# Second MLP product of the token mixer in five stretches per half, more output projections inside the attention loop, and the last attention units in pairs

## The chip, the cores and the metric

The kernel runs on one core of a Trainium2 chip. The metric is the device time of one execution in microseconds (us); smaller is better. A profiled execution also leaves a trace of every instruction of the five engines: TensorE (PE, with its weight loads as PEld), VectorE (DVE), ScalarE (ACT), GpSimd (POOL) and SyncE (SP, which starts nearly all DMAs here).

## The reference

```python
g = sigmoid((x * gate_w).sum(-1))                    # x: 2048 tokens x 640
# A: attention, 32 heads of 20, one key and value head for all
q = (x @ wq) -> 32 heads x 2048 x 20;  k = x @ wk;  v = x @ wv      # 2048 x 20
p = softmax(q k^T / sqrt(20)) over 2048 keys
a = concat_heads(p v) @ wo                           # 2048 x 640
# B: mixer MLP over the token axis, for each of 640 channels
h = layernorm(x)                                     # over channels
u = gelu(h^T w1 + b1)                                # 640 x 1728
b = (u w2 + b2)^T                                    # 2048 x 640
out = g * a + (1 - g) * b                            # all float32
```

## The kernel before, in words

**Precision.** Large products are made in three fp32r products of a high and a low part (high*high, high*low, low*high), so each block product is three matmuls. Splitting a tile into its parts is a copy (high) and a subtraction (low).

**Attention.** 2048 queries x 32 heads are cut into 32 groups n (512 queries, 4 heads); each group has 16 key blocks kb of 128 keys. A pair (n, kb) is a unit; there are 512. For a unit TensorE makes four score tiles of 128 keys x 512 queries (`qk`, L655, "s"), ScalarE takes the exponential of each (L658, tile p), and `pv_mm` (L682) multiplies the four p with the values into one PSUM bank o, four heads side by side as column tiles of 32. Ahead of that, every group needs the maximum of each query's scores: TensorE makes the scores a second time with queries on the partitions (`ms_next`, L474, "m") and VectorE reduces each 512-wide tile (L477). The maxima go through DRAM back into two rows of the q tile (`store_max`, `fetch_max`).

Score products need 60 or 62 of 128 rows of the array, so each uses one half of the rows, 0 to 63 or 64 to 127.

**The loop of stretches.** The list `ph` has 326 entries; `main(k, vs)` issues one, called a stretch here. Stretch k has b = k % 2. Half b of the array rows makes scores ("s" and "m", 10 or 11), while the other half makes fillers: the matmuls of 64 rows x 320 columns of the MLP and of the output projection, with an "m" or two at the end or beginning. `merged` lays the two lists together by fixed guesses (0.232 and 0.147 us). A stretch closes with the value products of one unit (k even) or two units (k odd), which use all rows. With more than 15 fillers a stretch follows the lists `MANY` (11 score products on half b), with 15 or fewer `FEW` (10 in the one-unit stretches, 11 in the two-unit ones, with one m more on the other half). Where the first unit of a two-unit stretch is the last key block of its group, its value products are put in the middle of the stretch (`parted`).

The fillers of one item (one output tile of 128 x 320) accumulate in the single PSUM bank g. Before the fillers of the other row half may write there, a one-element VectorE memset (`flag`, L668) signals that those of the last stretch are done. After the last filler of an item ScalarE takes the bank out (`done`: L514 in the first MLP product, L749 in the second, L869 in the projection).

- Stretches 0 to 107: first MLP product, 18 items of 6 stretches, 16 fillers in each (the first ten items ran before the loop).
- Stretches 108 to 299: second MLP product (`b2_jobs`, L741), 16 token blocks x 2 channel halves d. The sum runs over 1728 = 13 x 128 + 64 rows of w2. A product of 128 rows is two fillers, one in each half of the array; the 64 rows left over go to either half. That makes 81 fillers per item, in 6 stretches of 13 or 14.
- Stretches 300 to 325: output projection (`a_jobs`, L856) of 6.5 of the 16 token blocks, 15 fillers in each stretch.

**What a finished group leaves to do.** `pv_mm` of key block 15 copies the bank o to SBUF (ScalarE, L695, tile oc) and queues steps in `later`: `scale` (a VectorE transpose L698, "turn", a reciprocal L703 and a GpSimd product), `back` (VectorE transpose L710), `high` and `low` (GpSimd, then eight DMAs to o_scr). `settle` takes one step at a time. The two heavy ones, `scale` and `back`, are taken only by `settle(wide)` with wide true, at the end of a two-unit stretch.

**The tail.** After the loop 24 units are left, with no maxima to make. They run in the blocks of `BLOCKS`: each issues scores up to 2 (block of 3) or 4 (block of 2) tiles beyond its own units, with fillers (`tail_job`, L812) between, and then the value products of its units in a row. The fillers are the projections that the loop did not do: 5.5 whole blocks and, for the last four token blocks, the rows of the heads that are done. Scores use three PSUM banks and the p tiles are 14 here. The last four heads' part of the last four blocks follows at the end.

**Queues.** All engines run in the order in which the program issues (manual schedule). SP starts all loads and stores in order; the w2 chunks (four per token block, `w1_load`) are loaded four chunks ahead, and GpSimd splits them (L124, L125) when `w1_upto` asks for it, in four pairs of tiles that the next block reuses. Tail loads (`tail_load`) go to SP too.

Of the kernel before, what the change touches and what calls it, by code (L numbers as in the profile page):

```python
# [17 lines left out]
P = 128  # L18
# [13 lines left out]
BLOCKS = (3, 3, 2, 3, 3, 3, 3, 2, 2)  # L32
# [6 lines left out]
def mix_kernel(ctx: ExitStack, tc: tile.TileContext, A_x, A_wq, A_wk, A_wv, A_wo,  # L39
# [51 lines left out]
    def w1_load(n):  # L91
        while len(w1raw) < min(n, len(chunks)):
            c = len(w1raw)
            wr = w1r.tile([P, HS, P], F32, name="wr")
            if c < W2:
                fc, hf = chunks[c]
                rows = slice(hf * HS * P, (hf + 1) * HS * P)
                for o in range(0, P, P if fc < FC - 1 else FT):
                    fw = P if fc < FC - 1 else FT
                    nc.sync.dma_start(out=wr[:, :, o:o + fw],  # L100
                                      in_=B_w1[rows, fc * P:fc * P + fw].rearrange("(c p) f -> p c f", p=P))
            else:
                st, hf = chunks[c]
                cols = slice(st * P, (st + 1) * P)
                nf = min(HS, FC - 1 - hf * HS)
                nc.sync.dma_start(out=wr[:, :nf, :],
                                  in_=B_w2[hf * HS * P:(hf * HS + nf) * P, cols].rearrange("(c p) s -> p c s", p=P))
                if nf < HS:
                    for o in range(0, P, FT):
                        nc.sync.dma_start(out=wr[o:o + FT, nf, :], in_=B_w2[(FC - 1) * P:, cols])  # L110
            w1raw[c] = wr

    def w1_upto(n):
        while fetched[0] < min(n, len(chunks)):
            c = fetched[0]
            w1_load(c + 1)
            nf = HS if c < W2 else min(HS, FC - chunks[c][1] * HS)
            wr = w1raw[c][:, :nf, :]
            wh = w1p.tile([P, HS, P], F32R, name="wh")[:, :nf, :]
            wl = w1p.tile([P, HS, P], F32R, name="wl")[:, :nf, :]  # L120
# [319 lines left out]
    u0 = upool.tile([P, 2 * FC * HD2], F32R, name="u0")  # L440
    u_hi = [view(t, 0, FC) for t in (u0, slot[0])]
    u_lo = [view(t, FC * HD2, FC) for t in (u0, slot[0])]
    pp_pool = ctx.enter_context(tc.tile_pool(name="pp", bufs=12))
# [166 lines left out]
    def second():  # L610
        right.close()
        xp = ctx.enter_context(tc.tile_pool(name="xp", bufs=1, side="right"))
        extra_p.extend(xp.tile([P, NB], F32, name=f"p{i}") for i in range(2))
# [22 lines left out]
    def next_p():  # L636
        turn_p[0] += spare[0]
        i = turn_p[0] % 14
        return extra_p[i - 1] if 0 < i < 3 else pp_pool.tile([P, NB], F32, name="p")
# [36 lines left out]
    def pv_mm(u):  # L676
# [7 lines left out]
        if kb == NS - 1:  # L684
# [8 lines left out]
            if not direct:  # L693
                src = ev.tile([P, NB], F32, name="oc")
# [35 lines left out]

    def b2_jobs(st):
# [26 lines left out]

        return (lambda: None), [(steps(d), lambda d=d: done(d)) for d in range(2)]
# [16 lines left out]
    NA = NS - 9  # L776
    jobs = [(st, 0, D) for st in range(NA - 1, NS - 4)]
# [22 lines left out]
    def tail_job(n):  # L800
# [3 lines left out]
        ds = (1,) if st < NA else (0, 1)  # L804
# [33 lines left out]
    def a_jobs(st):  # L838
        hold = {}
        ds = (0,) if st == NA - 1 else (0, 1)  # L840
# [97 lines left out]
    b2 = [b2_jobs(st) for st in range(NS)]  # L938
    m = len(seq)
    seq += batches(b2, [3] * 2 * NS)  # L940
    for st in range(NS - 1):
        for j, n in ((0, 1), (1, 2), (2, 4)):
            seq[m + 6 * st + 3 + j][1].append(lambda c=W2 + 4 * (st + 1) + n: w1_upto(c))
    seq[-1][1].append(second)
    for c in range(DC):
        seq[m + 9 + 8 * c][1].append(lambda c=c: load_wo(c))
        seq[m + 11 + 8 * c][1].append(lambda c=c: split_wo(c))
    aj = [a_jobs(st) for st in range(NA)]
    seq[-6][1].append(aj[0][0])
    seq += batches(aj, [1] * (2 * NA - 1))  # L950
    ph = [(rows[1 - b], rest if b else [], done if b else []) for rows, rest, done in seq for b in range(2)]
    for i in range(8):
        ph[2 * (m + 6 * NS) + 2 + 3 * i][1].append(lambda i=i: tail_load(i))
# [30 lines left out]
    def main(k, vs):  # L984
# [25 lines left out]
        settle(wide)  # L1010
# [28 lines left out]
    for n in BLOCKS:  # L1039
# [29 lines left out]
        while len(loaded) < len(jobs) and len(loaded) - 8 not in waiting and (len(loaded) < 10 or v >= 501):  # L1069
# [61 lines left out]
```

## Time and profile before

| | before |
|---|---|
| time, median of 3 runs (lowest to highest) | 1690.6 us (1690.49 to 1690.65) |
| the profiled execution's own time | 1690.12 us |
| its span, first to last instruction | 1688.3 us |
| loop, first to last flag (326 stretches) | 182.9 to 1598.4 us |
| stretches 108 to 299, second MLP product | 654.3 to 1490.2 us |
| busy: PE, DVE, ACT, POOL | 99%, 86%, 70%, 34% of the span |

The span is 1.8 us shorter than the execution, which holds what lies before the first and behind the last instruction. The ends of matmuls are modelled, so the busy share of PE says only that it always has something in flight; how well it is used is read from the distance between starts. The flag memset stands once in each stretch, so the times of the flags cut the loop into stretches.

### The profile page before, as it was taken

How to read it: one execution, taken by the hardware profiler on the slowest of the kernel's cores; microseconds unless marked ns; L12 is line 12 of the kernel's file. 1: busy time of each engine (PE TensorE's matmuls, PEld its weight loads, DVE VectorE, ACT ScalarE, POOL GpSimd, SP SyncE). 2: the span in 40 equal slices, each digit the busy share in tenths (PEclk: the TensorE clock that was granted, in tenths of full speed). 3: DMA queues.
4: the chain of work that ended last, by engine and by line, in shares of the span. 5: the costliest groups of instructions: out<-in, count | busy, mean ns of one | idle time of the engine just before them, and what ended most of it. 6: DMA issues, size and time to landing. Idle time of an engine off the chain costs nothing.

```text
span 1688.3 us, 38969 instructions
## 1 busy us (share of the span) xinstructions
PE 1677.0 (99%) x14865; PEld 1098.7 (65%) x14865; DVE 1444.0 (86%) x2759; ACT 1189.0 (70%) x2349; POOL 571.4 (34%) x720
## 2 busy tenths in 40 slices
PE   9999999999999999999999999999999999999998
PEld 7899766666666666665655665565666566566676
DVE  6679889988998998998898999889889889989824
ACT  4444677777777777777777777777777777777764
POOL 6468555544555553221122212222211222011200
PEclk9999999999999999999999999999999999999999
DMA  7665322223232231121222212121112221255521
GB/s 210 203 181 145 84 68 69 77 64 83 59 77 77 59 76 55 51 67 41 63 70 59 62 39 68 56 62 55 39 54 57 60 63 33 56 141 162 150 91 45
DMA packets 174977, 136.44 MB, mean 81 GB/s; under 512 B 32793, under 2 KB 140982, under 8 KB 174790
## 3 DMA queue, kind: packets, MB, share of 16 engines
q1 hardware_dynamic: 174502, 133.62, 28.6%
q8 instruction: 117, 1.92, 0.5%
q14 instruction: 70, 0.57, 0.1%
q10 hardware_dynamic: 288, 0.33, 0.1%
HBM read 101.25 MB, written 31.65 MB: 79 GB/s over the span
## 4 chain that ended last, share of the span: by engine, by line
PE 94%; DVE 3%; issue 2%; SPq 1%; DMA 0%; ACT 0%; POOL 0%; POOLq 0%; DVEq 0%; ACTq 0%
PE o L682 28%; PE ms L474 12%; PE s L655 12%; PE g L741 10%; PE ms L655 9%; PE s L474 7%; PE g L910 6%; PE pp L294 4%; PE pu L584 3%; PE g L856 1%; DVE mp L477 1%; PE ms L812 1%; PE pt L286 0%; DVE ot L698 0%; PE g L812 0%
## 5 line engine op out<-in xcount | busy, mean ns | idle before, releaser
L477 DVE TENSOR_REDUCE mp<-ms 128x1 f32<-128x512 f32 x1081 | 708.8, 686 | 112.8 <-PE ms L474 94.4
L658 ACT ACTIVATE p<-s 128x512 f32<-128x512 f32 x1079 | 610.4, 615 | 200.7 <-PE s L655 145.9
L477 DVE TENSOR_REDUCE mp<-s 128x1 f32<-128x512 f32 x967 | 634.0, 683 | 38.5 <-PE s L474 38.4
L658 ACT ACTIVATE p<-ms 128x512 f32<-128x512 f32 x969 | 542.0, 607 | 168.5 <-PE ms L655 140.9
L682 PE MATMUL o<-p,v_sb 128*32 128x512 f32 x4096 | 510.7, 600 | 0.0
L474 PE MATMUL ms<-kst,qmx 60*128 60x512 f32 x1081 | 460.0, 435 | 0.6 <-DVE mp L477 0.4
L655 PE MATMUL s<-qst,kst 62*128 62x512 f32 x1079 | 445.0, 418 | 3.5 <-DVE mp L477 3.5
L474 PE MATMUL s<-kst,qmx 60*128 60x512 f32 x967 | 402.5, 433 | 0.4 <-DVE yo L520 0.4
L655 PE MATMUL ms<-qst,kst 62*128 62x512 f32 x969 | 401.7, 415 | 0.5 <-DVE mp L477 0.5
L655 PEld LDWEIGHTS s<-qst,kst 62*128 62x128 f32 x1079 | 197.9, 185 | 128.0 <-DVE flag L668 91.4
L474 PEld LDWEIGHTS ms<-kst,qmx 60*128 60x128 f32 x1081 | 198.1, 184 | 126.0 <-ACT p L658 67.9
L910 PE MATMUL g<-slot,wh 64*128 64x320 f32 x1152 | 268.5, 312 | 0.0
L655 PEld LDWEIGHTS ms<-qst,kst 62*128 62x128 f32 x969 | 179.7, 185 | 98.1 <-issue 60.4
L125 POOL TENSOR_TENSOR wl<-wr,wh 128x512 fp32r<-128x512 f32 (+1 forms) x176 | 221.8, 1263 | 32.7 <-ACT wh L122 21.6
L682 PEld LDWEIGHTS o<-p,v_sb 128*32 128x32 f32 x4096 | 97.8, 108 | 184.4 <-issue 176.5
L741 PE MATMUL g<-slot,wh 64*128 64x320 f32 x864 | 208.7, 313 | 0.0
L741 PE MATMUL g<-u,wh 64*128 64x320 f32 x864 | 208.6, 313 | 0.0
L910 PEld LDWEIGHTS g<-slot,wh 64*128 64x128 f32 x1152 | 190.6, 184 | 2.0 <-issue 1.7
L474 PEld LDWEIGHTS s<-kst,qmx 60*128 60x128 f32 x967 | 179.0, 185 | 17.2 <-DVE mp L477 14.1
L910 PE MATMUL g<-slot,wl 64*128 64x320 f32 x576 | 180.0, 313 | 0.0
L704 POOL TENSOR_TENSOR ot<-ot,rl 128x512 f32<-128x512 f32 x30 | 31.5, 1052 | 425.5 <-DVE rl L703 425.5
L124 POOL CAST wh<-wr 128x512 fp32r<-128x512 f32 (+1 forms) x136 | 80.2, 590 | 203.9 <-PE g L741 104.1
(205 smaller groups left out, 2207.1 us busy)
## 6 DMA issues: line engine op xcount, KB each, us to landing
wr<-in_B_w_dram SPq DMA_DIRECT2D x152, 256.0 KB
qmx<-q_scr SPq DMA_DIRECT2D x192, 80.0 KB
qst<-q_scr SPq DMA_DIRECT2D x192, 80.0 KB
slot<-o_scr SPq DMA_DIRECT2D x18, 320.0 KB
y_scr<-yo SPq DMA_DIRECT2D x16, 320.0 KB
o_scr<-oh SPq DMA_DIRECT2D x124, 40.0 KB
o_scr<-ol SPq DMA_DIRECT2D x124, 40.0 KB
q_scr<-qh SPq DMA_DIRECT2D x19, 256.0 KB
```

The source lines that it names most:

```text
L124: nc.gpsimd.tensor_copy(wh, wr)
L125: nc.gpsimd.tensor_sub(wl, wr, f32(wh))
L294: nc.tensor.matmul(pp, w, t, start=first and n == 0, stop=not more and n == len(steps) - 1)
L474: nc.tensor.matmul(ms, qmax[n][64 * b:64 * b + 60, pr, qt * P:(qt + 1) * P], kst[64 * b:64 * b + 60, kq * NB:(kq + 1) * NB], start=True, s ...
L477: nc.vector.tensor_reduce(mtiles[n][:, c, kq:kq + 1], ms, axis=AX.X, op=ALU.max)
L584: nc.tensor.matmul(pu[r][:, :HD2], w[rows, c, :], h[rows, st, :], start=(st == 0 and k == 0), stop=(st == NS - 1 and k == 2))
L655: nc.tensor.matmul(s, kst[64 * b:64 * b + 62, kb * P:(kb + 1) * P], q[64 * b:64 * b + 62, pr, :], start=True, stop=True)
L658: nc.scalar.activation(p, s, AF.Exp, scale=SCALE)
L682: nc.tensor.matmul(o[32 * hh:32 * hh + 32, :], v_sb[:, kb, :], ptiles.pop((u, hh)), start=(kb == 0), stop=(kb == NS - 1), skip_group_check ...
L704: (nc.vector if spare[0] else nc.gpsimd).tensor_mul(ot, ot, rl[:, :, None].to_broadcast([P, NB // 32, 32]))
L741: other_tile(half, nc.tensor.matmul(hold["p"][:, :HD2], w[r, fc % HS, :], u[d][r, fc, :], start=(hold["n"] == 1), stop=(hold["n"] == 6 * F ...
L910: other_tile(half, nc.tensor.matmul(hold["p"][:, :HD2], w[r, st % HS, :], h[d][r, st, :], start=(hold["n"] == 1), stop=(hold["n"] == 6 * NS)))
```

## The change

- **Five stretches.** For the first `FIVE` = 7 token blocks the second MLP product takes five stretches per item where it took six. So that fillers can be dealt unevenly to the row halves, two row blocks (fc 0 and 1, 256 rows of w2) are kept in both halves: `w1_load` loads their rows once more, swapped, into the free places 14 and 15 of the last chunk, and `twin_u` copies the two u blocks to the other half by DMA (four DMAs, in the first stretch and 20 stretches ahead of the second product). The stretches of an item take 16, 17, 16, 16 and 16 fillers, alternately on one half and the other; so they follow `MANY`, the item of d = 0 ends in a one-unit stretch (k even), and that of d = 1 starts in a two-unit one. The chunk of the last rows is now split as a whole tile.
- **More projections in the loop.** The 14 stretches so freed, with the 26 at the end, take ten token blocks' output projection (`NA` = 10) in place of 6.5. The loop keeps 326 stretches, and all steps that hang on a stretch's number (`load_wo`, `split_wo`) keep theirs. The tail has 300 fillers in place of 510. Tail loads: six, two stretches apart, from 13 stretches before the end, in place of eight, three apart.
- **The tail in pairs.** `BLOCKS` is twelve blocks of two units, in place of (3, 3, 2, 3, 3, 3, 3, 2, 2).
- **The parted stretch.** It ends with `settle(wide and not parted)`: `scale` is not taken there but at the end of the next two-unit stretch.
- **Tiles.** The copy of o goes to `on` and the tile oc is gone; p tiles of the loop are 11 in place of 12, three in place of two are added for the tail; u0 is larger by two row blocks in both parts.

```diff
-BLOCKS = (3, 3, 2, 3, 3, 3, 3, 2, 2)
+BLOCKS = (2,) * 12
+NA = 10
...
+                if hf == 3:
+                    for h in range(2):
+                        nc.sync.dma_start(out=wr[64 * (1 - h):64 * (2 - h), 2:, :],
+                                          in_=B_w2[:2 * P, cols].rearrange("(c h p) s -> h p c s", c=2, h=2)[h])
...
-            if not direct:
-                src = ev.tile([P, NB], F32, name="oc")
+            if not direct:
+                src = on
                 nc.scalar.activation(src, o, AF.Copy)
...
+    FIVE = 6 * NS - (163 - 3 * (2 * FC - PRO) - 2 * NA)
+
+    def twin_u(d):
+        for t in (u_hi[d], u_lo[d]):
+            h = 64 * d
+            nc.sync.dma_start(out=f32(t)[64 - h:128 - h, FC:, :], in_=f32(t)[h:64 + h, :2, :])
...
+        def five(d):
+            most = [(fc, k) for fc in range(UC) for k in range(3)]
+            few = [(fc, k) for fc in range(2, FC - 1) for k in range(3)]
+            parts = most[:16], few[:17], most[16:32], few[17:], most[32:]
+            out = [([lambda fc=fc, k=k, h=(1 - d + i) % 2: mm(fc, k, d, h) for fc, k in p], [], [])
+                   for i, p in enumerate(parts)]
+            out[-1][2].append(lambda: done(d))
+            return out
...
+    ph[m - 20][1].append(lambda: twin_u(1))
+    for st in range(NS):
+        job = b2_jobs(st)
+        if st < FIVE:
+            for d in range(2):
+                at = len(ph)
+                ph += job[d]
+        else:
+            at = len(ph) + 6
+            ph += stretches(batches([job], [3] * 2))
+        if st < NS - 1:
+            for k, n in ((at + 1, 1), (at + 3, 2), (len(ph) - 1, 4)):
+                ph[k][1].append(lambda c=W2 + 4 * (st + 1) + n: w1_upto(c))
...
-        settle(wide)
+        settle(wide and not parted)
...
-        while len(loaded) < len(jobs) and len(loaded) - 8 not in waiting and (len(loaded) < 10 or v >= 501):
+        while len(loaded) < len(jobs) and len(loaded) - 8 not in waiting and v >= 501:
```

Line numbers in the changed file are larger by 5 (L668 is L673 there) up to the second MLP product, and by 12 to 22 behind it (L741 is L753, L749 is L761, L812 is L834, L856 is L878).

**TensorE where the bank g changes from one channel half to the other** (first token block of the second product). u is the first half's operand, slot the second's; o are value products, x8 a pair of units, x4 one. Before:

```order
L741 MATMUL g<-u_1162,wl 128x320
L474 MATMUL ms<-kst,qmx 128x512
L741 MATMUL g<-u_1162,wh 128x320
L474 MATMUL s<-kst,qmx 128x512
L741 MATMUL g<-u_1162,wl 128x320
L474 MATMUL ms<-kst,qmx 128x512
L474 MATMUL s<-kst,qmx 128x512
L682 MATMUL o<-p,v_sb 32x512 x8
L655 MATMUL ms<-qst,kst 128x512
L741 MATMUL g<-slot_82,wh 128x320 x2
L474 MATMUL s<-kst,qmx 128x512
```

The change:

```order
L753 MATMUL g<-u_1162,wh 128x320 x2
L660 MATMUL s<-qst,kst 128x512
L753 MATMUL g<-u_1162,wl 128x320
L479 MATMUL ms<-kst,qmx 128x512
L479 MATMUL s<-kst,qmx 128x512
L687 MATMUL o<-p,v_sb 32x512 x4
L479 MATMUL ms<-kst,qmx 128x512
L753 MATMUL g<-slot_82,wh 128x320 x2
L660 MATMUL s<-qst,kst 128x512
```

Between the last filler of the one half and the first of the other there are now the value products of one unit, where there were those of two.

**VectorE around the first parted stretch**, in the first MLP product. ot<-oc and ot<-on are the turn, rl the reciprocal, flag closes a stretch. Before:

```order
L668 MEMSET flag 1x1
L477 TENSOR_REDUCE mp<-s 128x1
L698 STREAM_TRANSPOSE ot<-oc 128x512
L703 RECIPROCAL rl<-ot 128x16
L477 TENSOR_REDUCE mp<-ms 128x1 x5
L668 MEMSET flag 1x1
L477 TENSOR_REDUCE mp<-s 128x1
L477 TENSOR_REDUCE mp<-ms 128x1 x5
L668 MEMSET flag 1x1
```

The change:

```order
L673 MEMSET flag 1x1
L482 TENSOR_REDUCE mp<-s 128x1
L482 TENSOR_REDUCE mp<-ms 128x1 x5
L673 MEMSET flag 1x1
L482 TENSOR_REDUCE mp<-s 128x1
L482 TENSOR_REDUCE mp<-ms 128x1 x5
L673 MEMSET flag 1x1
L482 TENSOR_REDUCE mp<-s 128x1
L703 STREAM_TRANSPOSE ot<-on 128x512
L708 RECIPROCAL rl<-ot 128x16
```

The first flag of each list is that of the parted stretch. The turn and the reciprocal stand two stretches later.

**TensorE in the tail.** s are scores, o value products, L812 and L834 fillers. Before, the end of the first block, of three units, and the start of the second:

```order
L812 MATMUL ms<-slot_83,u_1162 128x320
L812 MATMUL g<-slot_83,u_1162 128x320
L812 MATMUL ms<-slot_83,u_1162 128x320
L812 MATMUL g<-slot_83,u_1162 128x320
L812 MATMUL ms<-slot_83,u_1162 128x320 x10
L682 MATMUL o<-p_24364,v_sb 32x512
L682 MATMUL o<-p,v_sb 32x512
L682 MATMUL o<-p_24365,v_sb 32x512
L682 MATMUL o<-p,v_sb 32x512 x9
L655 MATMUL s<-qst,kst 128x512 x3
L812 MATMUL ms<-slot_83,u_1162 128x320 x11
```

The change, a whole block of two:

```order
L660 MATMUL s<-qst,kst 128x512 x3
L834 MATMUL g<-slot_83,u_1162 128x320 x2
L834 MATMUL ms<-slot_83,u_1162 128x320 x9
L660 MATMUL s<-qst,kst 128x512
L834 MATMUL ms<-slot_83,u_1162 128x320 x5
L660 MATMUL s<-qst,kst 128x512
L834 MATMUL ms<-slot_83,u_1162 128x320 x5
L660 MATMUL s<-qst,kst 128x512
L834 MATMUL ms<-slot_83,u_1162 128x320 x3
L660 MATMUL s<-qst,kst 128x512 x2
L834 MATMUL ms<-slot_83,u_1162 128x320
L687 MATMUL o<-p,v_sb 32x512 x8
```

The run of value products is eight where it was twelve; the block has eight scores and 25 fillers, of which one stands behind the last score, where the block of three had 14 and more behind it.

More of the change, by code (lines that the diff above doesn't have):

```diff
@@ L116, in w1_upto @@
             w1_load(c + 1)
[L117 to L120, printed above, removed]
+            wr = w1raw[c]
+            wh = w1p.tile([P, HS, P], F32R, name="wh")
+            wl = w1p.tile([P, HS, P], F32R, name="wl")
             if c < 4 * PRO:
@@ L439, in mix_kernel @@
     upool = ctx.enter_context(tc.tile_pool(name="upool", bufs=1))
[L440 to L443, printed above, removed]
+    UC = FC + 2
+    u0 = upool.tile([P, 2 * UC * HD2], F32R, name="u0")
+    u_hi = [view(t, 0, UC) for t in (u0, slot[0])]
+    u_lo = [view(t, UC * HD2, UC) for t in (u0, slot[0])]
+    pp_pool = ctx.enter_context(tc.tile_pool(name="pp", bufs=11))
     ev = ctx.enter_context(tc.tile_pool(name="ev", bufs=1))
@@ L757, in steps @@
                     for f in full + [[(FC - 1, 0), (FC - 1, 1)], [(FC - 1, 2)]]]
+        def five(d):
[7 more added lines that the diff above has]
+        if st < FIVE:
+            return [five(d) for d in range(2)]
         return (lambda: None), [(steps(d), lambda d=d: done(d)) for d in range(2)]
@@ L937, in mix_kernel, with stretches @@
         rest.insert(0, lambda c=4 * (PRO + item) + (48 * j // 3) // 12: w1_upto(c + 4))
[L938 to L944, printed above, removed]
+    def stretches(seq):
+        return [(rows[1 - b], rest if b else [], done if b else []) for rows, rest, done in seq for b in range(2)]
+    ph = stretches(seq)
+    ph[0][1].append(lambda: twin_u(0))
+    m = len(ph)
+    ph[m - 20][1].append(lambda: twin_u(1))
+    for st in range(NS):
+        job = b2_jobs(st)
+        if st < FIVE:
+            for d in range(2):
[7 more added lines that the diff above has]
+                ph[k][1].append(lambda c=W2 + 4 * (st + 1) + n: w1_upto(c))
+    ph[-1][1].append(second)
     for c in range(DC):
[L946 to L947 removed]
+        ph[m + 19 + 16 * c][1].append(lambda c=c: load_wo(c))
+        ph[m + 23 + 16 * c][1].append(lambda c=c: split_wo(c))
     aj = [a_jobs(st) for st in range(NA)]
[L949 to L953, printed above, removed]
+    ph[-12][1].append(aj[0][0])
+    ph += stretches(batches(aj, [1] * 2 * NA))
+    assert len(ph) == 326
+    early = NS - 4 - NA + 4
+    for i in range(early):
+        ph[len(ph) - 3 - 2 * (early - 1 - i)][1].append(lambda i=i: tail_load(i))
     X_US, F_US, EXP_US = 0.232, 0.147, 0.477
```

11 lines of the change are left out of this document (5 added, 6 removed).

## Prediction

> **What bounds the kernel now.** I read the page first. The span and the busy shares:
>
> ```profile
> span 1688.3 us, 38969 instructions
> ...
> PE 1677.0 (99%) x14865; PEld 1098.7 (65%) x14865; DVE 1444.0 (86%) x2759; ACT 1189.0 (70%) x2349; POOL 571.4 (34%) x720
> ...
> PEclk9999999999999999999999999999999999999999
> ```
>
> TensorE is never without work, and its granted clock never leaves full speed, so no clock effect is in play. Next, the busy time of each engine in three stages of the loop and in the tail (columns: stretch, length, then PE, PEld, DVE, ACT, POOL, the clock, the DMA share, GB/s):
>
> ```profile
> 187.00:654.00 467.00, 466.53 (x4284) 301.83 (x4280) 420.17 (x798) 355.16 (x708) 234.05 (x305) 1.00 0.27 68
> ...
> 959.00:1490.00 531.00, 528.73 (x4577) 319.32 (x4577) 475.04 (x910) 391.08 (x766) 108.74 (x147) 1.00 0.20 55
> 1490.00:1598.00 108.00, 108.00 (x975) 69.29 (x971) 97.43 (x187) 82.56 (x166) 22.34 (x29) 1.00 0.58 166
> 1598.00:1676.00 78.00, 77.67 (x811) 54.89 (x803) 28.16 (x55) 47.06 (x95) 3.41 (x6) 1.00 0.19 59
> ```
>
> The first row is the first MLP product, the second most of the second, the third the projection, the fourth the tail. In the loop DVE has 420.17 of 467 us and 475.04 of 531: close behind TensorE. In the tail it falls to 28.16 of 78, and ACT, which should have only exponentials to do there, is at 47.06 of 78. So the tail waits somewhere that the loop does not. The flags give the mean length of a stretch (count, then the first and last start):
>
> ```profile
> L668 DVE MEMSET flag<- x108: 59/59/59, 187.1 to 654.3; 1x1 f32 x108
> L668 DVE MEMSET flag<- x71: 59/59/59, 654.3 to 958.8; 1x1 f32 x71
> L668 DVE MEMSET flag<- x26: 59/59/59, 1490.2 to 1598.4; 1x1 f32 x26
> ```
>
> First product: (654.3 - 187.1)/107 = 4.366 us with 16 fillers. Second: (958.8 - 654.3)/70 = 4.350 with 13 or 14. Projection: (1598.4 - 1490.2)/25 = 4.328 with 15. Three more fillers in a stretch cost 0.02 us: the time hangs on something else. TensorE's own timeline of one two-unit and one one-unit stretch of the first product shows on what:
>
> ```profile
> 409.80 1.07 PE L682 MATMUL o<-p,v_sb 128*32 128x512 f32 x8
> 410.79 0.49 PE L474 MATMUL ms<-kst,qmx 60*128 60x512 f32 x1
> ...
> 411.05 0.31 PE L910 MATMUL g<-slot,wh 64*128 64x320 f32 x1
> 411.13 0.39 PE L655 MATMUL s<-qst,kst 62*128 62x512 f32 x1
> ...
> 413.11 0.30 PE L910 MATMUL g<-slot,wl 64*128 64x320 f32 x1
> 413.26 0.50 PE L474 MATMUL ms<-kst,qmx 60*128 60x512 f32 x1
> 413.27 0.49 PE L474 MATMUL s<-kst,qmx 60*128 60x512 f32 x1
> 413.69 1.92 PE L682 MATMUL o<-p,v_sb 128*32 128x512 f32 x16
> 415.55 0.50 PE L474 MATMUL ms<-kst,qmx 60*128 60x512 f32 x1
> ...
> 418.46 1.07 PE L682 MATMUL o<-p,v_sb 128*32 128x512 f32 x8
> 419.45 0.50 PE L474 MATMUL ms<-kst,qmx 60*128 60x512 f32 x1
> ```
>
> Scores start 0.237 us apart (the second at 411.13, the eleventh at 413.26), fillers beside them 0.147 apart (the second at 411.05, the sixteenth at 413.11). The sixteenth filler's slot ends at 413.26, just as the eleventh score starts; the filler half's last m goes beside that score, at 413.27. The change to value products costs 0.42 (413.27 to 413.69), and from one unit's value products to the next score it is 0.99 (418.46 to 419.45). The two stretches take 4.76 and 3.90, 8.66 as a pair; a second unit costs their difference, 0.86. So a stretch is 11 scores in a row, then value products; 16 fillers fit beside the scores.
>
> **The change part by part.** *Longer fillers.* Seven blocks x 10 stretches become of the 16-filler kind, at 4.366 for 4.350: 70 x 0.016 = +1.1 us. The 17th filler of 14 of them has no room: in program order it stands between the eleventh score and the filler half's last m, and delays that by one pitch: 14 x 0.147 = +2.1 (bounds 0 and 2.1).
>
> *The item that ends in a one-unit stretch.* Seven times the bank g must be emptied behind one unit's value products instead of two. The emptying lasts 0.662, and it stands behind six exponentials, of which the last two are these:
>
> ```profile
> L741 PEld LDWEIGHTS g<-u,wh 64*128 64x128 f32 x864 | 147.4, 184 | 0.5
> ...
> L749 ACT ACTIVATE yo<-g,b2g,og_half 128x320 f32<-128x320 f32 x32 | 21.2, 662 | 0.0
> ```
>
> ```profile
> 418.25 1.12 ACT L658 ACTIVATE p<-s 128x512 f32<-128x512 f32 x2
> ```
>
> At 0.495 an exponential (from the tail's rows below, (5.99 - 5.00)/2) ACT is free at 418.25 + 0.99 = 419.24, the bank at 419.90. TensorE's next stretch started at 419.45, with a filler as its second instruction, and scores queue behind it in order. Stall 0.45, x 7 = +3.2 (bounds 0, if ACT is ahead there, and 7 x 0.99 = 7).
>
> The Trainium skill, "TensorE: Matmul & The Clock Gate", Part 3, "The mechanism", says that weight loads overlap matmuls in flight only where the row group differs. Were that so here, a run of fillers in one half could not be 0.147 apart, since the load alone is 184 ns in the row above; the trace disagrees, and by that rule the change would be the last rival below.
>
> *The parted stretch.* There are ten (stretch 11 and every 32nd). Two undisturbed stretches of the second product, then the parted one with its follower, then the same pair in the first product, all on DVE:
>
> ```profile
> 727.65 0.06 DVE L668 MEMSET flag<- 1x1 f32 x1
> ...
> 736.26 0.06 DVE L668 MEMSET flag<- 1x1 f32 x1
> ```
>
> ```profile
> 783.90 0.06 DVE L668 MEMSET flag<- 1x1 f32 x1
> ...
> 789.30 0.06 DVE L668 MEMSET flag<- 1x1 f32 x1
> ...
> 790.48 0.70 DVE L698 STREAM_TRANSPOSE ot<-oc 128x512 f32<-128x512 f32 x1
> 791.22 0.25 DVE L703 RECIPROCAL rl<-ot 128x16 f32<-128x16 f32 x1
> ...
> 793.75 0.06 DVE L668 MEMSET flag<- 1x1 f32 x1
> ```
>
> ```profile
> 226.68 0.06 DVE L668 MEMSET flag<- 1x1 f32 x1
> ...
> 236.29 0.06 DVE L668 MEMSET flag<- 1x1 f32 x1
> ```
>
> The first product's pair takes 9.61 for 8.66, so 0.95 more; the second's 793.75 - 783.90 = 9.85 for 736.26 - 727.65 = 8.61, so 1.24 more. Part of it is the additional change to value products and back: 0.42 + 0.99 - 0.86 - 0.24 = 0.31, which stays. The rest, 0.64 and 0.93, I put down to the turn and reciprocal (790.48 to 791.39, 0.9) at the start of the follower. A parted stretch leaves DVE behind, with reductions to catch up, and the follower has only one unit of value products to do it in; the banks are not freed and TensorE stands. Two stretches later DVE has caught up. That is where two of three turns stand already, and the stage means contain them. With 0.05 off for the new place: six parted stretches now run beside 16 fillers (four in the first product, two in the five-stretch blocks), four beside fewer: 6 x 0.6 + 4 x 0.9 = -7.2 (bounds 0 and -8.1 - 0.2 for rounding). What waits for the turn is the group's store to o_scr, two stretches later; the last parted stretch is number 299, and the first load that needs its rows is given at stretch 317, so no one is held up.
>
> *Fourteen stretches of projection* in place of as many of the second product: 14 x (4.328 - 4.350) = -0.3, which I take as 0, since no parted stretch lies in the projection now.
>
> *The rest, at nothing.* Four copy DMAs and two more loads per chunk of last rows stand on SP ahead of loads that run four chunks in advance; the split of a whole tile is GpSimd's, which is busy 108.74 of 531 us there; one p tile fewer still covers the 11 that are live before a two-unit stretch's value products. The six tail loads come closer together, behind and ahead of the projection's own loads; if one projection load lands late it costs a few us once. If all this cover went, a chunk would be late seven times, at a us or two each.
>
> *The tail.* The exponentials in runs, one a block, and the last value products:
>
> ```profile
> 1600.02 5.49 ACT L658 ACTIVATE p<-s 128x512 f32<-128x512 f32 x11 [1.48 <-PE s L655]
> 1609.39 5.99 ACT L658 ACTIVATE p<-s 128x512 f32<-128x512 f32 x12 [3.88 <-PE s L655]
> 1618.80 5.00 ACT L658 ACTIVATE p<-s 128x512 f32<-128x512 f32 x10 [3.42 <-PE s L655]
> 1625.27 5.01 ACT L658 ACTIVATE p<-s 128x512 f32<-128x512 f32 x10 [1.46 <-PE s L655]
> ...
> 1662.69 5.00 ACT L658 ACTIVATE p<-s 128x512 f32<-128x512 f32 x10 [3.28 <-PE s L655]
> 1669.16 2.07 ACT L658 ACTIVATE p<-s 128x512 f32<-128x512 f32 x4 [1.47 <-PE s L655]
> ```
>
> ```profile
> 1674.18 1.92 PE L682 MATMUL o<-p,v_sb 128*32 128x512 f32 x16
> ```
>
> A block of three (12 exponentials) takes 1618.80 - 1609.39 = 9.41 us, a block of two with ten 6.47 (1662.69 to 1669.16, and 1618.80 to 1625.27 the same). ACT works 5.00 of 6.47 and then waits for scores, since scores wait behind the value products. With twelve pairs all blocks but the first and last have eight: 6.47 - 2 x 0.495 = 5.48. Fillers fit: four scores and 12 fillers in a half are 4 x 0.237 + 12 x 0.147 = 2.7, in 5.48 - 0.99 - 0.86 = 3.6. In the long blocks before they did not: the run of 12 ends at 1615.38, and its value products start only with the fillers done. From the first exponential to the last value products: first block (nine) 5.97, ten at 5.48, and the last one, bounded by its four exponentials (2.4) and by the last block of before (5.02 from 1669.16 to 1674.18, 47 fillers): 31 fillers, 3.3. Sum 64.1, against 1674.18 - 1600.02 = 74.2: -10.1 (bounds -6 to -13, if the step per exponential is 0.3 or 0.6 rather than 0.495). What follows the last value products is the same work.
>
> Sum: 1.1 + 2.1 + 3.2 - 7.2 - 10.1 = -10.9. The profiled execution took 1690.12, 0.5 below the median of the runs; from the median, 1690.6 - 10.9 = **1679.7**.
>
> **The rivals.** *The stall of the parted stretch does not go with the turn* (10%). If the missing slack comes from the value products being parted, and the turn only happens to lie there, then 7.2 us stay: 1686.9. For it: DVE still has to wait while the parted unit's value products keep TensorE from making scores. Against it: the 0.64 and 0.93 are about the 0.9 of turn and reciprocal, and the plain turns show no such price in the mean.
>
> *Pairs stay at 6.47* (7%), because a block's price is the changes between scores and value products and not its exponentials; then the tail is 11 x 0.99 = 10.9 longer than I say, and the whole 1690.6, no change. For it: twelve runs of value products in place of nine. Against it: the block of 12 costs 9.41 - 6.47 = 2.94 more for one unit (0.86) and two exponentials, and a change costs 0.31 by the rows above, 0.9 for three more. The Trainium skill, "TensorEngine Tiling (Array Packing)", "Key Properties", says that a change of the tiling mode drains the array, without a figure; the trace agrees with its 0.31, and by that rule alone the smaller blocks speak against the change.
>
> *The filler half sets the pace of the five-stretch blocks* (5%), and the kernel is slower. The place is the 70 stretches. The filler half has no slack, so each 0.01 more in the pitch of 15 costs 0.15 a stretch; at 0.184, the weight load's duration, a stretch loses 15 x 0.037 = 0.56, in all 39: 1719. It decides from a pitch of 0.158, where 10.9/70 = 0.16 a stretch eats the gain. Against it stand the 108 stretches of the first product with 16 fillers, 0.147 apart.
>
> **How the numbers follow.** My forecast has 78%, rivals 10, 7 and 5. About 0.2%, 3.4 us, is what a measurement can tell here, so 1687.2 is the edge of "same". The forecast lies well below it, at its own bounds too: with fillers and emptying at nothing 1674.4, with all at the worst some 1686. The first rival lies on the edge and gives half its chance to each side; the second is the same, the third slower: faster 0.83, same 0.12, slower 0.05. The range, 1674 to 1688, holds the forecast with its bounds and the first rival.
>
> **What would show it.** Right: last value products about 64 us behind the tail's first exponential, with runs of eight exponentials 5.5 apart; the loop from first to last flag 1 us shorter than 1415.5, with 4.4 to 4.5 a stretch in the first seven blocks; a pair of 8.9 to 9.1 where a parted stretch stands, no turn in the follower; TensorE waiting 0.4 for the emptied bank seven times. Wrong: pairs 6 us apart or more; a pair of 9.6 with the turn gone; TensorE waiting for GpSimd's chunks in the first blocks of the second product; fillers more than 0.15 apart.

## The result and the profile after

The changed kernel takes 1677.7 us (median of four runs, 1677.42 to 1678.3) against 1690.59 us before (1690.49 to 1690.65): ratio 0.9924, 95% interval 0.9907 to 0.9941. It is 12.9 us faster, where 10.9 were forecast; 1677.7 lies in the range and 2.0 below the predicted 1679.7.

The page of the kernel after, its first part:

```profile
span 1675.9 us, 38869 instructions
...
PE 1668.3 (100%) x14865; PEld 1102.7 (66%) x14865; DVE 1440.1 (86%) x2745; ACT 1193.4 (71%) x2356; POOL 588.4 (35%) x727
...
PEclk9999999999999999999999999999999999999999
```

The same number of matmuls lies in a span that is 12.4 us shorter, at the same clock: work was laid closer together, none went away. The window of the tail, columns as before:

```profile
1597.00:1664.00 67.00, 66.80 (x595) 39.71 (x588) 19.94 (x40) 46.83 (x93) 3.03 (x6) 1.00 0.11 32
```

In the tail ACT now works 46.83 of 67 us, where it was 47.06 of 78: the same exponentials in less time. The flags of the first product and of the five-stretch blocks:

```profile
L673 DVE MEMSET flag<- x108: 59/59/59, 187.4 to 653.2; 1x1 f32 x108
```

```profile
L673 DVE MEMSET flag<- x70: 59/59/59, 653.2 to 957.2; 1x1 f32 x70
```

(653.2 - 187.4)/107 = 4.353 us a stretch for 4.366, and (957.2 - 653.2)/69 = 4.406 in the five-stretch blocks, inside the 4.4 to 4.5 forecast. The first and last flag of the loop are 1413.2 apart (183.19 to 1596.43), 2.2 less than before. The tail, ACT's exponentials and the last value products:

```profile
1598.02 4.51 ACT L663 ACTIVATE p<-s 128x512 f32<-128x512 f32 x9 [1.48 <-PE s L660]
...
1620.19 4.03 ACT L663 ACTIVATE p<-s 128x512 f32<-128x512 f32 x8 [1.39 <-PE s L660]
1625.76 4.03 ACT L663 ACTIVATE p<-s 128x512 f32<-128x512 f32 x8 [1.54 <-PE s L660]
1631.18 4.03 ACT L663 ACTIVATE p<-s 128x512 f32<-128x512 f32 x8 [1.40 <-PE s L660]
```

```profile
1661.78 1.92 PE L687 MATMUL o<-p,v_sb 128*32 128x512 f32 x16
```

A pair takes 5.57 (1625.76 - 1620.19) or 5.42, where 5.48 was forecast. From the first exponential to the last value products it is 63.76 us for 74.16, so -10.4. Loop and tail give -12.6 of the span's -12.4; the first flag is 0.3 later. What the numbers do not say is why the tail is shorter and why the loop has become shorter by more than forecast. The experiments are about these two.

### The profile page after: what moved, and what is told of

Its sections match the earlier page's. It is cut to its first block, busy times and chain, and to the rows that moved or that the text cites. A ratio compares the mean times of both kernels' runs of the same rounds, so it can differ in the third digit from the quotient of the medians.

```text
span 1675.9 us, 38869 instructions
## 1 busy us (share of the span) xinstructions
PE 1668.3 (100%) x14865; PEld 1102.7 (66%) x14865; DVE 1440.1 (86%) x2745; ACT 1193.4 (71%) x2356; POOL 588.4 (35%) x727
## 3 DMA queue, kind: packets, MB, share of 16 engines
q8 instruction: 117, 1.92, 0.5%
## 4 chain that ended last, share of the span: by engine, by line
PE 95%; issue 2%; DVE 1%; SPq 1%; ACT 0%; DMA 0%; POOL 0%; POOLq 0%; DVEq 0%; ACTq 0%
PE o L687 28%; PE ms L479 15%; PE s L660 12%; PE g L753 10%; PE ms L660 7%; PE g L932 6%; PE s L479 5%; PE pp L298 4%; PE pu L589 3%; PE g L878 2%; DVE mp L482 1%; PE ms L834 0%; PE pt L290 0%; ACT p L663 0%; SPq L195 0%
## 5 line engine op out<-in xcount | busy, mean ns | idle before, releaser
L482 DVE TENSOR_REDUCE mp<-ms 128x1 f32<-128x512 f32 x1298 | 839.3, 685 | 122.3 <-PE ms L479 97.8
L663 ACT ACTIVATE p<-s 128x512 f32<-128x512 f32 x1296 | 714.8, 607 | 241.0 <-PE s L660 205.5
L479 PE MATMUL ms<-kst,qmx 60*128 60x512 f32 x1298 | 552.4, 433 | 0.7 <-DVE mp L482 0.5
L482 DVE TENSOR_REDUCE mp<-s 128x1 f32<-128x512 f32 x750 | 493.2, 682 | 23.3 <-PE s L479 23.0
L663 ACT ACTIVATE p<-ms 128x512 f32<-128x512 f32 x752 | 420.7, 602 | 112.3 <-PE ms L660 96.5
L479 PE MATMUL s<-kst,qmx 60*128 60x512 f32 x750 | 311.8, 429 | 0.4 <-DVE yo L525 0.4
L660 PE MATMUL ms<-qst,kst 62*128 62x512 f32 x752 | 308.6, 410 | 0.0
L129 POOL TENSOR_TENSOR wl<-wr,wh 128x512 fp32r<-128x512 f32 x176 | 230.5, 1312 | 42.9 <-ACT wh L126 21.7
L753 PE MATMUL g<-slot,wh 64*128 64x320 f32 x864 | 205.1, 313 | 0.0
L753 PE MATMUL g<-u,wh 64*128 64x320 f32 x864 | 205.0, 313 | 0.0
L932 PEld LDWEIGHTS g<-slot,wh 64*128 64x128 f32 x1152 | 190.7, 184 | 2.0 <-issue 1.7
L128 POOL CAST wh<-wr 128x512 fp32r<-128x512 f32 x136 | 83.4, 613 | 187.6 <-PE g L753 67.4
L753 PEld LDWEIGHTS g<-slot,wh 64*128 64x128 f32 x864 | 145.1, 184 | 2.4 <-ACT yo L761 2.1
```

The lines of the kernel that those rows point to most:

```text
L128: nc.gpsimd.tensor_copy(wh, wr)
L129: nc.gpsimd.tensor_sub(wl, wr, f32(wh))
L479: nc.tensor.matmul(ms, qmax[n][64 * b:64 * b + 60, pr, qt * P:(qt + 1) * P], kst[64 * b:64 * b + 60, kq * NB:(kq + 1) * NB], start=True, s ...
L482: nc.vector.tensor_reduce(mtiles[n][:, c, kq:kq + 1], ms, axis=AX.X, op=ALU.max)
L660: nc.tensor.matmul(s, kst[64 * b:64 * b + 62, kb * P:(kb + 1) * P], q[64 * b:64 * b + 62, pr, :], start=True, stop=True)
L663: nc.scalar.activation(p, s, AF.Exp, scale=SCALE)
```

## Experiments

**Theories.** Theory A: the tail is shorter because 300 fillers stand in it instead of 510; blocks of two have no part in it. Theory B: it is shorter because blocks of two make two exponentials fewer than the old blocks of two did, as the prediction's sum had it. For the loop, the theory is the prediction's (the turn made the parted stretch's follower stall), and the rival is its first rival (the parted value products did). Each expectation states its own rival. Before's median on the chips of the experiments was 1690.31 to 1690.63, and the ratios stand to that.

**The turn, back in its old place**, in the kernel after:

```diff
-        settle(wide and not parted)
+        settle(wide)
```

> The changed kernel with scale taken at the end of the parted stretch again, as before. Theory (the turn at the start of the follower makes the stall): each of the ten parted stretches loses what it had won, 0.65 us beside 16 fillers and 0.85 beside fewer, 6 x 0.65 + 4 x 0.85 = 7.3 in all: 1677.7 + 7.3 = 1685. Rival (the stall went for another reason: the copy of o in another tile, 11 p tiles, other fillers): within 1 us of 1677.7.

Measured: 1683.85 us (1683.13 to 1684.16), ratio 0.9961 (0.9946 to 0.9976), so +6.1. VectorE in this run, flags around the first parted stretch, with the turn and reciprocal in its follower:

```profile
227.76 0.06 DVE L673 MEMSET flag<- 1x1 f32 x1
...
232.84 0.06 DVE L673 MEMSET flag<- 1x1 f32 x1
233.43 0.70 DVE L703 STREAM_TRANSPOSE ot<-on 128x512 f32<-128x512 f32 x1
...
237.38 0.06 DVE L673 MEMSET flag<- 1x1 f32 x1
```

and in the kernel after, without them there:

```profile
226.93 0.06 DVE L673 MEMSET flag<- 1x1 f32 x1
...
232.01 0.06 DVE L673 MEMSET flag<- 1x1 f32 x1
...
235.95 0.06 DVE L673 MEMSET flag<- 1x1 f32 x1
```

The parted stretch takes 5.08 in both; the follower takes 4.54 with the turn and 3.94 without. What the edit moves is the step `scale`, which is the turn, the reciprocal and the GpSimd product. So the stall belongs to the place of that step; the parted value products stand in the same place in both runs.

**The turn alone moved**, in the kernel before:

```diff
-        settle(wide)
+        settle(wide and not parted)
```

> The kernel before with the one change that scale is not taken at the end of a parted stretch. Theory: four parted stretches beside 16 fillers win 0.65, six beside 13 or 14 win 0.85: 7.7, so 1690.6 - 7.7 = 1682.9. Rival (the stall went for another reason): 1690.6.

Measured: 1683.76 (1683.41 to 1686.68), ratio 0.9966 (0.9953 to 0.9979), so -6.6. The profiled execution took 1686.68, so I take the median for the time and the trace only for the pairs. The stretch that the prediction showed, TensorE in the kernel before:

```profile
791.17 0.30 PE L741 MATMUL g<-slot,wh 64*128 64x320 f32 x1
792.07 0.49 PE L655 MATMUL s<-qst,kst 62*128 62x512 f32 x1 [0.60 <-DVE mp L477]
```

and VectorE with the turn moved:

```profile
781.96 0.06 DVE L668 MEMSET flag<- 1x1 f32 x1
...
787.35 0.06 DVE L668 MEMSET flag<- 1x1 f32 x1
...
790.95 0.06 DVE L668 MEMSET flag<- 1x1 f32 x1
...
796.38 0.70 DVE L698 STREAM_TRANSPOSE ot<-oc 128x512 f32<-128x512 f32 x1
```

Before, a score waits 0.60 us for a bank that VectorE has not reduced yet. With the turn moved the pair takes 790.95 - 781.96 = 8.99 for 9.85, and the turn stands behind the next two-unit stretch. Summed over the ten parted stretches, the pairs are 7.39 shorter; the two stretches behind them, where the turn now stands, are 1.34 longer, and the two after those 0.67 shorter. That is -6.7, as the median has it. The move costs 0.07 a turn where it lands. The loop of this trace is only 3.6 shorter than before's, because of one pair in the projection:

```profile
1521.59 0.47 PE L655 MATMUL ms<-qst,kst 62*128 62x512 f32 x1 [1.92 <-DMA qst<-m_scr]
```

A score waits 1.92 us there for its group's maxima, the granted clock from 1520 to 1525 us is 0.69 (1.00 in the kernel before), and the pair takes 12.05 for 8.89. Why the maxima came late is open.

**The old blocks in the kernel after:**

```diff
-BLOCKS = (2,) * 12
+BLOCKS = (3, 3, 2, 3, 3, 3, 3, 2, 2)
```

> The changed kernel with the old blocks of three and two units in the tail, and 300 fillers as it has. Theory A (a block lasts as long as its exponentials and value products, and what made the old blocks long were 510 fillers): a block of three with 12 exponentials takes 5.49 + 0.86 + 4 x 0.485 = 8.3 instead of 9.4, one of two with ten 6.47, and the tail from first exponential to last value products is 64.5 for 63.8: 1678.4. Theory B (pairs are what shortens the tail): the blocks of three keep 9.4 us, the tail goes back to some 74: 1688.

Measured: 1677.92 (1677.82 to 1678.4), ratio 0.9926 (0.9910 to 0.9943): the time of the kernel after. ACT in this run:

```profile
1605.89 5.99 ACT L663 ACTIVATE p<-s 128x512 f32<-128x512 f32 x12 [2.46 <-PE s L660]
1614.19 5.01 ACT L663 ACTIVATE p<-s 128x512 f32<-128x512 f32 x10 [2.31 <-PE s L660]
1620.59 5.00 ACT L663 ACTIVATE p<-s 128x512 f32<-128x512 f32 x10 [1.40 <-PE s L660]
```

A block of three takes 8.30 where it took 9.41 with 510 fillers; the block of two with ten exponentials takes 6.40 for 6.47. So the fillers had made the long blocks longer and the block of two hardly. Theory B falls: with 300 fillers the old blocks are as fast as pairs within the spread of the runs.

**Pairs in the kernel before**, with its 510 fillers: the same edit of `BLOCKS` the other way, to twelve twos.

> The kernel before with twelve pairs in the tail and its 510 fillers. Theory A (fillers): 21 fillers and four scores in a half, 21.25 x 0.147 + 4 x 0.237 = 4.07 us, no longer fit into the 3.64 between a pair's first score and its value products; a pair takes about 6 us, the tail some 70 for 74: 1686. Theory B (pairs): the tail falls to 64 as in the changed kernel: 1680.5.

Measured: 1690.68 (1690.31 to 1690.99), ratio 1.0002 (0.9993 to 1.0011): no change, where theory A gave 1686 and theory B 1680.5. ACT:

```profile
1632.20 4.03 ACT L658 ACTIVATE p<-s 128x512 f32<-128x512 f32 x8 [2.37 <-PE s L655]
1638.60 4.03 ACT L658 ACTIVATE p<-s 128x512 f32<-128x512 f32 x8 [2.37 <-PE s L655]
```

A pair takes 6.40, and ACT idles 2.37 of it. 510/12 = 42.5 fillers a pair are 21 in a half, 21 x 0.147 + 4 x 0.237 = 4.0; with the change to value products (0.42) and the two units (0.86 + 0.99) it makes 6.3. The end of such a pair on TensorE:

```profile
1635.01 0.39 PE L655 MATMUL s<-qst,kst 62*128 62x512 f32 x1
...
1635.53 0.75 PE L812 MATMUL ms<-slot,slot 64*128 64x320 f32 x7
1636.21 1.92 PE L682 MATMUL o<-p,v_sb 128*32 128x512 f32 x16
```

Between the last score and the value products stand 1.2 us of fillers alone. The filler half sets the pace. The expectation had put the pair near 6 because it left the change to the value products, 0.42, out of that half's time.

**Fewer and more projections in the loop** (`NA` = 9, 8 and 12 for 10): 360, 420 and 180 fillers in the tail, and five, three and eleven blocks of five stretches.

> The changed kernel with nine token blocks projected in the loop, so five blocks of the second product in five stretches instead of seven, and 360 fillers in the tail instead of 300. A block in five stretches costs 0.37 (wait for the bank) + 2 x 0.16 (17 fillers) + 5 x (8.66 - 8.59) = 1.0 us more than one in six, so the loop falls by 2.1. Theory A (a pair waits for its fillers only above a point): from the pairs with 510 fillers, 6.40 = 1.85 + 0.95 + 21.25 x 0.147 + 0.48, 15 fillers in a half give 1.85 + 0.95 + 2.2 + 0.48 = 5.48, no longer than now: 1675.6. Theory B (every filler in the tail costs its share of the 10.4 us that 210 fillers gave, 0.05): +3.0, 1678.6.

> The same with eight token blocks in the loop: three blocks in five stretches, 420 fillers in the tail. The loop falls by 4.2. Theory A: 17.5 fillers in a half give pairs of 1.85 + 0.95 + 2.57 + 0.48 = 5.85, 0.36 above the exponentials' 5.49, eleven times 4.0: 1677.5. Theory B: +6.0, 1679.5.

> The kernel after with twelve projections in the loop (eleven five-stretch blocks, 180 fillers in the tail). Theory: 300 fillers are already few enough that exponentials and banks set the pace of a pair, so the tail gets no shorter, and four more five-stretch blocks cost 4 x 1.04 = 4.2: about 1681.9. Rival (each filler out of the tail is worth 0.05 us all the way): 120 x 0.05 = 6 off the tail, 1675.9.

Measured: 1676.96 (1676.65 to 1677.94), ratio 0.9921 (0.9907 to 0.9936); 1679.46 (1679.02 to 1679.6), ratio 0.9935 (0.9920 to 0.9950); 1680.63 (1679.92 to 1681.49), ratio 0.9941 (0.9924 to 0.9958). All runs with blocks of two in one table, and the two with the old blocks; "tail" is from the first exponential to the last value products in each trace:

| fillers in the tail | blocks | tail, us | first to last flag, us |
|---|---|---|---|
| 510 (before) | old | 74.16 | 1415.47 |
| 510 (pairs in before) | twos | 74.54 | 1415.36 |
| 420 (`NA` = 8) | twos | 68.18 | 1410.54 |
| 360 (`NA` = 9) | twos | 65.02 | 1411.21 |
| 300 (after) | twos | 63.76 | 1413.24 |
| 300 (old blocks in after) | old | 64.55 | 1412.99 |
| 180 (`NA` = 12) | twos | 62.40 | 1417.02 |

From 510 to 420 a filler out of the tail is worth 6.36/90 = 0.071 us, which is about half of 0.147, as it should be where two halves share the fillers; from 300 to 180 it is worth 1.36/120 = 0.011. Between lies the corner, and it is not sharp: 0.053 from 420 to 360, 0.021 from 360 to 300. A projection more in the loop takes 60 fillers out of the tail and makes two more blocks of five stretches, which costs the loop 2.0 (nine to ten) or 1.9 (ten to twelve). From eight to nine it is only 0.7: the two blocks cost 2.4 where they stand, but further on single pairs of stretches are longer in the run with eight projections, for which no run shows the reason. From 420 fillers to 360 that pays, from 360 to 300 (1.26) it no longer does: nine projections are ahead of ten by 0.7, within the spread of their runs. With 420 fillers ACT's rows are

```profile
1636.33 4.03 ACT L663 ACTIVATE p<-s 128x512 f32<-128x512 f32 x8 [1.79 <-PE s L660]
1642.14 4.03 ACT L663 ACTIVATE p<-s 128x512 f32<-128x512 f32 x8 [1.79 <-PE s L660]
```

5.81, near theory A's 5.85. The times alone would mislead: 1679.46 is theory B's 1679.5 and not theory A's 1677.5, but the loop fell by 2.7 where both had counted on 4.2. The tail itself rose by 4.4 with 420 fillers (theory A 4.0, theory B 6.0), rose by 1.3 with 360 (0 and 3.0) and fell by 1.4 with 180 (0 and 6), each time nearer to theory A.

**What sets a pair when fillers no longer do.** TensorE in a pair of the kernel after, scores and value products only:

```profile
1619.66 0.50 PE L660 MATMUL s<-qst,kst 62*128 62x512 f32 x2
1620.00 0.39 PE L660 MATMUL s<-qst,kst 62*128 62x512 f32 x1
1620.87 0.47 PE L660 MATMUL s<-qst,kst 62*128 62x512 f32 x1
...
1621.90 0.41 PE L660 MATMUL s<-qst,kst 62*128 62x512 f32 x1
1622.31 0.98 PE L660 MATMUL s<-qst,kst 62*128 62x512 f32 x2
1623.37 1.92 PE L687 MATMUL o<-p,v_sb 128*32 128x512 f32 x16
```

Three scores go in a row, one to each bank of the tail; the fourth, at 1620.87, can only follow the first exponential (it starts at 1620.19), and from there scores come at ACT's 0.5. Two runs give a fourth bank, from the pool `ps_m` of three banks (not two, as one of the expectations has it) in which the fillers of the tail accumulate, beside the bank g; `% 4` or `% 8`:

```diff
+        tail_s[0] += spare[0]
-        s = ps_s.tile([P, NB], F32, name="s") if spare[0] else next_bank()
+        s = next_bank() if not spare[0] else (ps_s.tile([P, NB], F32, name="s") if tail_s[0] % 4
+                                              else ps_m.tile([P, NB], F32, name="ms"))
```

> The changed kernel with every fourth score of the tail in one of the three banks of the pool ms, so that four scores instead of three wait for ScalarE while the value products run. Theory A (a pair lasts as long as the eight exponentials less those that run during the value products): one more exponential is covered, 0.48 x 11 = 5.3 us less: 1672.4. Rival: the pool ms is then short for the fillers, TensorE waits for VectorE to empty the accumulators, and nothing is won: 1677 to 1680.

> The kernel after, with every eighth score tile of the tail taken from the two-buffer PSUM pool of the filler accumulators, so that a fourth bank helps once in a block of two. Theory (the tail's pairs wait for a score bank to be read, and one more bank in the place where the wait stands takes it away without a filler waiting for it): blocks fall from 5.42 and 5.57 to about 5.0, some 0.48 each, 11 x 0.48 = 5 us, 1672.5. Rival (the run with every fourth tile showed fillers that wait for the same pool; one in eight still meets that): as much is lost as won, 1677 to 1678.

Measured: every fourth 1678.77 (1678.14 to 1679.19), ratio 0.9931 (0.9914 to 0.9948), no gain; every eighth 1674.94 (1674.46 to 1675.22), ratio 0.9906 (0.9891 to 0.9921), 2.8 below the kernel after. With every fourth, TensorE shows what takes the gain back:

```profile
1653.89 0.41 PE L837 MATMUL ms<-slot,u 64*128 64x320 f32 x1 [0.54 <-ACT p L666]
...
1655.90 0.50 PE L663 MATMUL ms<-qst,kst 62*128 62x512 f32 x1 [0.50 <-DVE row L844]
```

A filler waits for the exponential that reads its bank, then a score for the filler's bank to be emptied. With every eighth, in a pair that loses (1616.91) and in one that does not:

```profile
1616.91 0.50 PE L663 MATMUL ms<-qst,kst 62*128 62x512 f32 x1 [0.47 <-DVE yo L844]
...
1634.83 0.50 PE L663 MATMUL s<-qst,kst 62*128 62x512 f32 x2
...
1637.43 0.46 PE L663 MATMUL ms<-qst,kst 62*128 62x512 f32 x1
...
1639.82 0.50 PE L663 MATMUL s<-qst,kst 62*128 62x512 f32 x2
```

In the second (1634.83 to 1639.82) the seventh score (ms) does not wait, and the pair takes 4.99. In the first it waits 0.47 for a filler's bank that VectorE has still to empty. Eight of the twelve pairs take 4.93 to 5.43; the other four, 5.45 to 5.76, and three of these hold such a wait. That is why the tail is 3.3 shorter (60.42), not the 5 expected. The mechanism is shown: the pair of the kernel after waits for score banks.

**The bank g emptied sooner.** In stretches of one unit that end an item the guess for a filler is made smaller, so that the emptying is issued ahead of the last exponential.

```diff
-        fill = [(F_US, f) for f in fs] + [(0.0, f) for f in [signal] + done]
+        f_us = 0.13 if done and len(vs) == 1 else F_US
+        fill = [(f_us, f) for f in fs] + [(0.0, f) for f in [signal] + done]
```

> The changed kernel with the fillers of the seven one-unit stretches that end an item laid as if each took 0.13 us, so that ScalarE empties the bank g ahead of the last exponential of that stretch. Theory (the wait of 0.37 at the start of the next stretch is ScalarE's place in its queue): the bank is free 0.48 earlier, the wait is gone, at most 0.1 is lost where scores wait for fillers: 7 x 0.3 = 2 us less, 1675.7. Rival (the wait is for the flag or for the change of halves): 1677.7.

Measured: 1677.02 (1676.39 to 1677.31), ratio 0.9920 (0.9906 to 0.9935), 0.7 below the kernel after where 2 were hoped for. The kernel after, TensorE at the first such end, and ACT's emptying:

```profile
667.11 0.50 PE L479 MATMUL ms<-kst,qmx 60*128 60x512 f32 x1
...
671.01 0.49 PE L479 MATMUL ms<-kst,qmx 60*128 60x512 f32 x1
671.50 0.41 PE L753 MATMUL g<-slot,wh 64*128 64x320 f32 x1
671.51 0.50 PE L660 MATMUL s<-qst,kst 62*128 62x512 f32 x1
```

```profile
670.81 0.64 ACT L761 ACTIVATE yo<-g,b2g,og_half 128x320 f32<-128x320 f32 x1
```

and with the emptying earlier:

```profile
670.73 0.63 ACT L761 ACTIVATE yo<-g,b2g,og_half 128x320 f32<-128x320 f32 x1
```

```profile
667.52 0.50 PE L479 MATMUL ms<-kst,qmx 60*128 60x512 f32 x1
...
671.64 0.50 PE L479 MATMUL ms<-kst,qmx 60*128 60x512 f32 x1
671.65 0.41 PE L753 MATMUL g<-slot,wh 64*128 64x320 f32 x1
```

The emptying starts 3.70 behind the start of its stretch in the kernel after (670.81 - 667.11) and 3.21 with the edit. In the kernel after the first filler comes 0.49 behind the first score, the second score directly behind it, and the two-unit stretch takes 5.13 (to 676.14) for 4.76. With the earlier emptying filler and score start together and that stretch is 4.76 again, but the one-unit stretch has grown from 3.90 (671.01 - 667.11) to 4.12: scores now stand behind fillers, 0.22 where at most 0.1 was expected. Net 0.15 of the 0.37; the loop is 0.9 shorter (1412.32 for 1413.24). So the theory has the wait right and its price too low.

**Both**, every eighth score and the earlier emptying:

> The run with one tile in eight, and with the emptying of the bank g ahead of the last exponential where an item ends in a one-unit stretch. The two lie in different stages and should add: 0.7 us below the run with one in eight alone, 1671.8 if that gives 1672.5, 1677 if it gives 1677.7.

Measured: 1673.86 (1673.14 to 1674.27), ratio 0.9900 (0.9885 to 0.9914), 1.1 below the run before it and 3.8 below the kernel after. They add within the spread of the runs, and this is the fastest version of the study.

**One p tile fewer**, in the kernel before. The loop had become shorter by more than its known terms, and the undisturbed pair of stretches in the six-stretch part had gone from 8.63 to 8.59 with nothing changed there but the tiles.

```diff
-    pp_pool = ctx.enter_context(tc.tile_pool(name="pp", bufs=12))
+    pp_pool = ctx.enter_context(tc.tile_pool(name="pp", bufs=11))
...
-        extra_p.extend(xp.tile([P, NB], F32, name=f"p{i}") for i in range(2))
+        extra_p.extend(xp.tile([P, NB], F32, name=f"p{i}") for i in range(3))
...
-        return extra_p[i - 1] if 0 < i < 3 else pp_pool.tile([P, NB], F32, name="p")
+        return extra_p[i - 1] if 0 < i < 4 else pp_pool.tile([P, NB], F32, name="p")
```

> The kernel before with 11 p tiles in the loop in place of 12 and three more for the tail in place of two. What is left of the loop's gain, about 1.5 us, shows as a pair of stretches of 4.97 + 3.62 in place of 5.00 + 3.63 in the six-stretch part. If the number of p tiles makes that, this run is 1.5 to 2 us faster than before, 1688.5 to 1689; if it does not, it is before's 1690.4, within 0.5.

Measured: 1687.03 (1686.8 to 1688.63), ratio 0.9981 (0.9972 to 0.9990): 3.6 faster by the medians, twice what was expected. In the traces the loop takes 1412.48 for 1415.47, 3.0 less, and the tail is unchanged (74.20). The exponentials' waits on ACT's queue, kernel before and this run:

```profile
L658 ACTq EVENT_SEMAPHORE  x675: 17/17/38, 182.7 to 1662.6; - x169
```

```profile
L658 ACTq EVENT_SEMAPHORE  x571: 17/17/38, 182.8 to 1659.7; - x191
```

104 separate waits are gone from ACT's queue: three more in the first product and 107 fewer behind it, about one for each of the 109 pairs of stretches there. The pair is 0.03 shorter there (the 102 pairs without a parted stretch take 8.636 on average, 8.607 in this run). Two pairs of the first product, at stretches 27 and 93, are longer instead: 8.88 for 8.66, and they are 8.86 to 8.88 in every kernel here with 11 tiles, the kernel after among them, and 8.65 or 8.66 in every one with 12. That the waits are the cause is argued, not shown: the number of tiles also shifts which exponential of a pair meets which tile, and where tiles lie.

## Why the prediction was right, and where not

**The parted stretch: right in mechanism and nearly in size.** Forecast -7.2; undone in the kernel after +6.1 (5.5 of it in the loop of the traces, where the loop also starts 0.8 later), done alone in the kernel before -6.6. The ten pairs of a parted stretch and its follower lost 6.9 between the kernels (96.7 to 89.8) and 7.4 with the turn alone, for the 7.6 that 6 x 0.64 + 4 x 0.93 gave. The 0.6 missing is about one pair: that of stretch 107, at the border to the second product, was counted with 0.64, but takes 8.94 before and 9.03 after. The new place takes back 0.07 a turn in the kernel before and 0.12 in the kernel after (its next four stretches, against those of the run with the turn back, 1.2 over ten), for the 0.05 deducted. The first rival (the stall stays) is refuted by both runs.

**The five-stretch blocks: right, and a little cheaper than forecast.** The second stretch of the first block, with the start of the next, on TensorE:

```profile
653.52 0.50 PE L479 MATMUL ms<-kst,qmx 60*128 60x512 f32 x1
...
658.44 0.50 PE L479 MATMUL ms<-kst,qmx 60*128 60x512 f32 x1
```

This two-unit stretch holds 17 fillers and takes 4.92 where 16 take 4.76: the 17th costs 0.16, forecast 0.147; the bank g emptied late 0.37, forecast 0.45. With 1.1 for the longer fillers that is 1.1 + 2.2 + 2.6 = +5.9, forecast +6.4. Inside an item the stretches of 16 fillers take 4.76 and 3.90 as in the first product, so the third rival did not occur.

**The loop as a whole: a term was missing.** The sum for the loop was -0.8 (1.1 + 2.1 + 3.2 - 7.2); measured -2.2. Three runs lead from the loop of before to that of after, one step each: 11 tiles alone (1415.47 to 1412.48), then everything else but the turn (the run with the turn back, 1418.71), then the turn (1413.24). The steps are -3.0, +6.2 and -5.5, where the prediction had 0, +6.4 and -7.2. In the 70 stretches of the five-stretch blocks the middle step is 308.97 for 303.05, the +5.9 of above. So the step that failed is "one p tile fewer still covers the 11 that are live", taken at nothing; that the turn gave 1.7 less hid more than half of it, which is luck. That the tiles do in the kernel after what they do in the kernel before is worked out from these runs, since the kernel after with 12 tiles was not run. For it speak the two pairs of 8.88 above and the waits on ACT's queue in the 148 stretches behind the five-stretch blocks: 372 before, 298 with 11 tiles and 298 in the kernel after.

**The tail: right in number and in the price of a pair, wrong about the long blocks.** Forecast -10.1, measured -10.4. The new tail came out term by term: the first block 5.91 (forecast 5.97), ten pairs of 5.42 or 5.57 (5.48), the last 3.05 (3.3). "6.47 - 2 x 0.495 = 5.48" holds: the block of two with ten exponentials takes 6.40 with 300 fillers as well, and 6.40 - 5.42 is two exponentials. What failed is the reading "the block of 12 costs 9.41 - 6.47 = 2.94 more for one unit (0.86) and two exponentials". With 300 fillers it costs 8.30 - 6.40 = 1.90 more, which is 0.86 + 2 x 0.495 = 1.85; the other 1.04 was fillers. The prediction had seen that fillers did not fit there, but not asked what the old blocks would take with 210 of them gone. They take 64.55 us in all, so the fillers are worth 9.6 of the 10.4 and the pairs at most 0.8, which does not show in the time (1677.92 for 1677.70). The sum came out because fewer fillers and pairs went into it together. The second rival (pairs stay at 6.47) was dismissed by the wrong argument: with 510 fillers pairs do stay, at 6.40, though the filler half sets that and not the changes that the rival named.

The mode changes that the second rival named do not show in the time either: three runs of value products more or fewer make 1677.70 and 1677.92. The Trainium skill, "TensorEngine Tiling (Array Packing)", "Key Properties", counts each change of mode as a drain; by that the old blocks should have been ahead by 3 x 0.31 = 0.9, and their tail was 0.8 longer.

**The 2.0 between forecast and result:** the loop 1.4 and the tail 0.3 better than said, the start 0.3 later, and 0.5 because the profiled execution of before was that much under its median and that of after was not. In us they add up to 1.9.

## What to carry to other kernels

A block that mixes several kinds of work has one pace, set by the longest of its chains; compute each chain (fillers in a half by their pitch, exponentials through the banks, value products) and take the largest, rather than adding the difference of two measured blocks, which holds only where the same chain sets both (6.47 and 5.42 here, but not 9.41). When a change moves two suspects at once (blocks and fillers here), the size of the effect cannot tell them apart, however well it fits; one run with each alone does. A buffer more is not always free: a run with one fewer tells its price, and the waits in the queue of the engine that uses it are a place to look.

## What had not been expected of the hardware

Eleven tiles instead of twelve for the exponentials' results make the kernel before 3.6 us faster, with 104 fewer separate wait instructions on ScalarE's queue. A fourth bank for the tail's scores shortens a pair from 5.42 to 4.93 us where no filler needs it, and is worth nothing when every fourth score takes it.
